# First loads interleaved with the modulation columns, W_v in quarters, two row norms on ScalarE, and a new seeded issue order

## The chip, the cores and the metric

The kernel runs on one core of a Trainium2 chip. The metric is the device time of one execution in microseconds (us). Five engines work side by side, each through its own queue in order: PE (TensorE: matmuls and transposes, with the weight loads shown as PEld), DVE (VectorE), ACT (ScalarE), POOL (GpSimd) and SP (SyncE, which here only issues DMAs). POOL and ACT issue some DMAs too.

## The reference

Two adaLN blocks on x of shape 1 x 2048 x 1024: linear attention (32 heads), then a gated feed-forward of inner size 3584. Both normalised inputs are scaled and shifted by rows that come out of the conditioning vector c.

```
mod = (silu(c) @ w_mod)            # six rows: sa, ca, ga, sb, cb, gb
h   = layernorm(x) * (1 + ca) + sa
q, k, v = h @ wqkv
o   = (phi(q) @ (phi(k)^T v)) / (phi(q) @ sum phi(k))   # per head, not causal
x   = x + ga * (o @ wo)
h   = layernorm(x) * (1 + cb) + sb
out = x + gb * (gelu(h @ w_gate) * (h @ w_up)) @ w_down
```

## The kernel before, in words

The 2048 rows are four blocks of 512, each of four row tiles of 128. Weights and rows are two-byte types. K and V of blocks 1 to 3, Q, and the feed-forward are computed with seven instead of eight block products (the helper `seven`, and lines L1492, L1503, L1698, L1742), so most of the vector work is sums of blocks (L672, a helper that all of them share).

Every instruction is first recorded by a `Plan`. PE keeps the order in which it was recorded. For DVE, ACT, POOL and SP the plan makes the order: it sweeps forwards and backwards over its own costs (`sweep`, `cost`), gives every instruction a due time, then shifts the due times of randomly chosen instructions, once for each number in `SEEDS` (`nudge`), and issues by due time. `plan.chain` makes a list of loads due in this order at the latest stage before the shifts; `plan.pairs` does so for two instructions; `aim` adds a wish without a wait.

The change sits in `start_phase`, block 0. It goes through these steps:

- **Loads** on SP: row tiles x0 to x3 (L665, 256 KB each); c (L660, 2 KB); the weights of the modulation row ca in four parts a0 to a3 (`ModRow`, L717, 512 KB each); W_v (L669) as two loads for its left half and one for its right half; the weights of row sa in four parts (L717); the left half of W_k (L669). Between them stand the row tiles x4 to x7 of block 1.
- **c chain**: transpose of c (L821), then silu of it on DVE and ACT (L822 to L825, L823, a product), and its spread over 32 columns, `srep` (L827).
- **Row norms** of the four tiles: `ln_stats` (two bn_stats, L750, and bn_aggr, L752, on DVE), `act_rstd` (L763, L764 on ACT), and the normalised rows `xh` (L771 on DVE).
- **Transposes** of each tile on PE (`start_tile`, L784), copied out of PSUM half by DVE (L787) and half by ACT (L788).
- **Modulation row ca**: four steps of four 32-column matmuls (L744), the row copied to SBUF (L730), turned into columns by four small matmuls (L735), and 1 added (L737, `opcA`).
- **V of block 0**: W_v scaled by `opcA` row by row (`scale_wv`, L792, eight instructions per half), `v_plain` (eight matmuls of 512 columns for one tile and one half, L799) and the copy out (L801). `psV0` hands out six PSUM banks in turn.
- **Row sa** the same way (L744, L730, L735, L737), then the scaled and shifted rows `hr1[0]` (L859) and the K products of block 0 (L1077).

`keep_warm` (L778) issues a matmul whose result nobody reads.

The recorded order on PE before is: transposes of tile 0, one keep_warm, ca step 0, transposes of tile 1, step 1, transposes of tile 2, steps 2 and 3, two keep_warm, the column matmuls, V left half of tiles 0 and 1, transposes of tile 3, V left half of tiles 2 and 3, V right half of tiles 0 and 1, the sa steps.

Of the kernel before, what the change touches and what calls it, by code (L numbers as in the profile page):

```python
# [24 lines left out]
class Plan:  # L25
# [170 lines left out]
    def sweep(self, back, key, look=False):  # L196
# [71 lines left out]
    PICK, NOISE = 21, 0  # L268
    SEEDS = (
        4048537842, 3052119424, 4119006662, 2336656596, 161731228, 3577097872, 1617916839, 1027230142,  # L270
        2673589267, 73385933, 3790190337, 2882579725, 3216820374, 320986960, 3784414771, 3580079639,
        2189647628, 1050075471, 3651447201, 167525183, 3753044056, 1395098839, 224573371, 585647736,
        4225116052, 2021886637, 2917317861, 1866056072, 1639904768, 1711702630, 3190854802, 40189043,
        2881217943, 3677486799, 3357445821, 867604809, 2076543648, 3896752996, 2934333674, 3357422997,
        3152768862, 640924042, 3205461639, 2011937210, 2000349924, 510719398, 2589235319, 1194506681,
        3024436697, 3992814688, 1998719246, 2949966658, 3489443318, 3776796425, 1276645235, 535667422,
        3611704417, 3250731288, 464907758, 1351614301, 2356189972, 234302744, 2220809080, 57131370, 642075108,
        2961538208, 2297863551, 4063326422, 2349725752, 2911337299, 1282626583, 2452324637, 621185154,
        7574608, 3707275484, 1951561619, 3730337220, 3301158178, 4291313931, 2153977638, 3028307953,
        3915374427, 2816343381, 3760783167, 781283501, 684728118, 501548599, 4094990745, 1484049200,  # L280
        2465562289, 3925350256, 965746493, 3646756344, 2285859381, 951057912, 2699291817, 1987664980,
        828984993, 2974115349, 2994019667, 2209336521, 2805814643, 1656178862, 2847076462, 974581971,
        2142746714, 1022025168, 2698599094, 1162505135, 294243250, 1388198210, 1320376692, 2717840438,
        1907634470, 1870354662, 3787058490, 2887567034, 731842052, 2849907486, 1949569065, 1725002371,
        3649967808, 2266963320, 1265187588, 320693273, 4133481684, 1239374557, 3322962508, 1823520108,
        922999944, 3964342922, 1626190444, 4021997209, 2818356799, 2606551328, 551488695, 2768152965,
        3756739242, 1178895203, 47899462, 2776984886, 1257449296, 978079115, 3512939827, 87745206, 2026573507,
        2193115765, 3542705403, 1987802722, 1329001258, 3298082478, 3301134813, 2791482809, 2941169553,
        2037818865, 1512528319, 2616816450, 362595370, 4022497973, 4049411141, 491327928, 2936576588,
        1810659750, 889849638, 4021601455, 3490155913, 707422581, 675677434, 1582781747, 3132129914,  # L290
        2734898311, 581041313, 3390668725, 1668609171, 617184354, 1308446589, 1521476646, 3271485029,
        188006670, 196406370, 1356859221, 673239658, 2473417458, 420321949, 3512578292, 2549304534,
        2893442801, 387476433, 320168298, 3725832190, 1491054289, 2258738015, 1870276432, 3456880632,
        2454290386, 3129029018, 697926410, 621392321, 2950830990, 3367784966, 1118316371, 2730688569,
        3949532447, 3051750465, 3325784910, 2506054308, 3860860484, 1996768650, 146936465, 1394849734,
        1876122295, 1648619962, 3935016806, 3537560656, 3783972569, 2354335454, 3477199748, 2926709925,
        16337124, 2717926436, 111481476, 3577080921, 1071120771, 2167836348, 4168772393, 3890589730,
        1077032086, 2081322183, 4253998603, 454015642, 4275186283, 4016079109, 3218202660, 304743196,
        2680513899, 3809773594, 567496057, 2830818904, 4138745561, 2171552190, 2973774733, 3221767405,
        3429062779, 1717540271, 22671747, 2877177301, 1539209414, 3279346260, 3479982363, 2042908008,  # L300
        2691901471, 1368355222, 326783083, 3723025629, 2456071862, 1765522499, 900449391, 1646784865,
        722122970, 3247420172, 144709712, 2707653883, 819893754, 3046126564, 2348285467, 1753457520,
        1370081680, 4241638063, 1889876362, 1719498627, 1097949531, 3059158255, 1826487528, 1087746401,
        1584062846, 450375441, 2497503536, 2423138386, 2114108004, 1214742892, 2086856895, 2411766887,
        2415497461, 1729688547, 1133947453, 3006387686, 18939909, 1126925613, 3055188306, 3624713728,
        1058512297, 2394622115, 3371373593, 178052737, 2641212401, 975232369, 1895527715, 3119219689,
        990010943, 2089507856, 2983971879, 996022692, 633189698, 1722843049, 1661576060, 1671655858,
        3182414464, 3582944425, 3047952838, 3254601484, 766187531, 914803382, 3727478657, 859608898,
        3197076401, 3401594207, 2518788814, 3045052436, 2880430921, 1855916904, 140371746, 1156500991,
        233814336, 3510688714, 4262759723, 1426092211, 3905079655, 2119269929, 2032944984, 3620558725,  # L310
        70133820, 3962811033, 754667546, 3073760965, 536237857, 4153583377, 4284871881, 273231253, 1032161433,
        3182043479, 2860624928, 2238869687, 1732234667, 1505353138, 2695169420, 1565396801, 3427962107,
        2673563735, 1099624156, 1397927899, 2237693769, 4118473817, 743005469, 3650425116, 2542140114,
        1153909673, 166372149, 3940934504, 2349500002, 3545793644, 410007833, 239392513, 894185139,
        1551465807, 1117651798, 1520533204, 20822420, 255004653, 438863435, 3129891357, 524023302, 4064637033,
        727558290, 1435463954, 53854510, 1999773738, 3466071934, 3199073121, 327427378, 1779665881,
        1915856973, 4162782897, 2466834344, 4248796843, 3211208784, 1624193377, 587107055, 1005140328,
        1097668263, 73267186, 3975834741, 3768422863, 2803021489, 2934859460, 2836787835, 2162329013,
        84326441, 3297589317, 913014749, 1570435363, 1768180507, 2744141746, 2458210240, 2303409726,
        786567120, 3437488657, 3085600183, 3596682727, 3241489828, 611671851, 4134240813, 1638792729,  # L320
        2540069415, 1263333970, 1713977921, 357095461, 642318044, 2476538737, 4111826224, 2345300137,
        3436573261, 2171236867, 3576962286, 4085290716, 1475585222, 3880589866, 4044342256, 3195652808,
        242737988, 3054416890, 1177578839, 3130838368, 4121588194, 29435970, 2881609414, 383494457, 726370357,
        90512414, 1561079870, 259102355, 1885219044, 2597283077, 909078396, 2293166713, 773209620, 717523002,
        1886363894, 2803820692, 507968540, 2979773247, 1603412096, 743301268, 3145502576, 2077775722,
        1338496569, 2126159865, 4004174970, 3665873461, 2555642967, 3607417742, 1860314205, 2467844904,
        1748351400, 3294511372, 1624161033, 11758325, 222342824, 1168818158, 1172645835, 3429412630,
        3380506841, 2739542149, 3442006596, 2772742892, 3321567846, 524445811, 364298885, 2556615645,
        2210968172, 2755680416, 1077432423, 4142317391, 2910697880, 2231545948, 1568488390, 2869103753,
        3579796744, 2673130065, 463737951, 1142281096, 2782314832, 2368998753, 1177439293, 2514790928,  # L330
        3029867465, 4224343348, 783400272, 2761726704, 1707892459, 3928657622, 2807650960, 992989999,
        4272533469, 3780895192, 3781928225, 200333331, 2996317106, 2825851012, 3989423859, 3739561707,
        3291555177, 1526625601, 1464234896, 2690896832, 3681443511, 713813461, 1057540405, 521674988,
        3204357066, 366938346, 2232734869, 2666123288, 707110826, 2810732530, 4204494926, 1885679090,
        1760645537, 1948061084, 2593472540, 1930019129, 1841665968, 2411340693, 4281658996, 2799186656,
        924293513, 1109206859, 3625276106, 3661854190, 1051793210, 235176749, 652886144, 3809779388,
# [68 lines left out]
def kernel(  # L405
# [305 lines left out]
    class ModRow:  # L711


        def __init__(self, m, wm, before={}):
            self.wm, self.ps, self.loads = wm, None, []
            for i in range(0, KD, 2):
# [3 lines left out]
                if i in before:  # L720
                    plan.aim(before[i])
# [1208 lines left out]
```

## Time and profile before

| what | us |
|---|---|
| median of 4 runs (lowest, highest) | 745.91 (745.42, 746.45) |
| the profiled execution | 744.84 |
| span of that execution, first to last instruction | 742.7 |
| PE busy in the span | 725.9 (98%) |
| DVE, ACT busy | 592.5 (80%), 433.1 (58%) |
| first V matmul of block 0 (L799) | at 16.38 |
| first sa step (L744 x16) | at 27.78 |
| first K product of block 0 (L1077) | at 32.32 |

Times in the tables and listings count from the start of the span. A timeline line gives start, duration, engine, source line, operation, out<-in, how many instructions it merges, and in brackets the idle time of the engine before it with what ended it. A window line gives busy time of each engine (and instruction counts), the granted PE clock, the DMA share and the GB/s that the DMA engines moved.

### The profile page before, as it was taken

How to read it: one execution, taken by the hardware profiler on the slowest of the kernel's cores; microseconds unless marked ns; L12 is line 12 of the kernel's file. 1: busy time of each engine (PE TensorE's matmuls, PEld its weight loads, DVE VectorE, ACT ScalarE, POOL GpSimd, SP SyncE). 2: the span in 40 equal slices, each digit the busy share in tenths (PEclk: the TensorE clock that was granted, in tenths of full speed). 3: DMA queues.
4: the chain of work that ended last, by engine and by line, in shares of the span. 5: the costliest groups of instructions: out<-in, count | busy, mean ns of one | idle time of the engine just before them, and what ended most of it. 6: DMA issues, size and time to landing. Idle time of an engine off the chain costs nothing.

```text
span 742.7 us, 11428 instructions
## 1 busy us (share of the span) xinstructions
PE 725.9 (98%) x4150; PEld 388.2 (52%) x4164; DVE 592.5 (80%) x1258; ACT 433.1 (58%) x757; POOL 95.0 (13%) x163
## 2 busy tenths in 40 slices
PE   4999999999999999999999999999999999999997
PEld 1444545444444455455455586545555555548664
DVE  6899987577785898698997888759788988888853
ACT  2665676669763769987876424027777777731000
POOL 2331335020001013242310000000000000000000
PEclk9999999999999999999999999999999999999999
DMA  9977159959999967998669998653231322499722
GB/s 307 330 211 226 61 144 205 312 148 277 281 273 254 340 209 251 296 242 260 193 191 236 238 264 265 228 183 125 75 114 57 113 73 99 134 280 285 291 85 71
DMA packets 151832, 152.79 MB, mean 206 GB/s; under 512 B 33824, under 2 KB 128544, under 8 KB 150496
## 3 DMA queue, kind: packets, MB, share of 16 engines
q1 hardware_dynamic: 128832, 122.44, 53.6%
q0 software_dynamic: 20592, 27.53, 15.8%
q10 hardware_dynamic: 2352, 2.10, 0.8%
q8 instruction: 32, 0.52, 0.3%
q14 instruction: 24, 0.20, 0.1%
HBM read 123.34 MB, written 36.04 MB: 215 GB/s over the span
## 4 chain that ended last, share of the span: by engine, by line
PE 93%; DVE 2%; DMA 2%; ACT 1%; issue 1%; SPq 0%; DVEq 0%
PE psum L1492 35%; PE psum L1698 13%; PE psum L1742 9%; PE psum L1503 8%; PE psum L978 8%; PE psum L1370 7%; PE psum L1048 5%; PE psum L1077 4%; PE psum L799 2%; DMA mem<-in_B_w_gate_dram 1%; PE psum L1092 1%; DVE mem L672 1%; DMA mem<-in_A_x_dram 1%; PE psum L689 0%; DVE mem L750 0%
## 5 line engine op out<-in xcount | busy, mean ns | idle before, releaser
L672 DVE TENSOR_TENSOR mem<-mem 128x512 f16<-128x512 f16 (+9 forms) x669 | 310.5, 506 | 31.6 <-ACT mem L923 11.9
L1492 PE MATMUL psum<-mem 128*128 128x512 f16 x1248 | 298.4, 379 | 0.2
L923 ACT ACTIVATE mem<-psum 128x512 f16<-128x512 f32 (+3 forms) x284 | 154.1, 563 | 111.0 <-PE psum L1742 39.8
L672 DVE TENSOR_TENSOR mem<-psum,mem 128x512 f16<-128x512 f32 (+4 forms) x204 | 154.9, 766 | 64.6 <-ACT mem L923 20.5
L1492 PEld LDWEIGHTS <-mem 128*128 128x128 f16 (+1 forms) x1248 | 122.1, 98 | 110.7 <-issue 0.7
L1698 PE MATMUL psum<-mem 128*128 128x512 f16 (+2 forms) x458 | 99.0, 372 | 0.7 <-DVE mem L672 0.5
L1503 PE MATMUL psum<-mem 128*128 128x256 f16 x560 | 89.6, 272 | 0.2 <-DVE psum L672 0.2
L1503 PEld LDWEIGHTS <-mem 128*128 128x128 f16 (+1 forms) x560 | 54.8, 98 | 44.4 <-issue 1.7
L1698 PEld LDWEIGHTS <-mem 128*128 128x128 f16 x462 | 45.2, 98 | 49.8 <-issue 0.7
L1742 PE MATMUL psum<-mem 128*128 128x256 f16 (+1 forms) x588 | 66.1, 273 | 0.0
L1742 PEld LDWEIGHTS <-mem 128*128 128x128 f16 x588 | 57.5, 98 | 9.2
L978 PE MATMUL psum<-mem 128*128 128x512 f16 (+1 forms) x272 | 61.6, 379 | 0.4
L1546 ACT ACTIVATE psum<-psum 128x512 f32<-128x512 f32 x56 | 32.8, 586 | 46.9 <-PE psum L1492 28.5
L1370 PE MATMUL psum<-mem 128*128 128x512 f16 x256 | 56.0, 379 | 0.0
L1048 PE MATMUL psum<-mem 128*128 128x512 f16 x224 | 51.2, 379 | 0.3 <-DVE mem L672 0.3
L672 DVE TENSOR_TENSOR psum<-psum,mem 128x256 f32<-128x256 f32 x80 | 34.3, 429 | 15.1 <-ACT mem L923 14.5
L978 PEld LDWEIGHTS <-mem 128*128 128x128 f16 x280 | 27.0, 98 | 31.2
L1370 PEld LDWEIGHTS <-mem 128*128 128x128 bf16 x256 | 24.8, 98 | 30.4 <-DVE mem L672 0.7
L1563 ACT ACTIVATE mem<-psum 128x512 f16<-128x512 f32 x56 | 32.6, 596 | 8.0 <-PE psum L1492 7.8
L1048 PEld LDWEIGHTS <-mem 128*128 128x128 f16 (+1 forms) x224 | 21.5, 98 | 27.7 <-issue 2.9
L1573 ACT ACTIVATE mem<-mem 128x512 f16<-128x512 f16 x56 | 34.5, 625 | 0.9 <-DVE mem L672 0.8
L1157 POOL DMA_DIRECT2D ts<-in_B_w_down_dram x28 | 31.3, 1469 | 11.6 <-DMA ts<-in_B_w_down_dram 11.2
(133 smaller groups left out, 526.0 us busy)
## 6 DMA issues: line engine op xcount, KB each, us to landing
mem<-in_B_w_gate_dram SPq DMA_DIRECT2D x14, 1024.0 KB, 5.2
mem<-in_B_w_up_dram SPq DMA_DIRECT2D x14, 1024.0 KB, 6.8
mem<-in_w_mod_dram SPq DMA_DIRECT2D x24, 512.0 KB, 6.3
mem<-ts SPq DMA_DIRECT2D x6, 1792.0 KB, 6.9
mem<-in_A_x_dram SPq DMA_DIRECT2D x32, 256.0 KB, 7.6
ts<-in_B_w_down_dram POOLq DMA_DIRECT2D x28, 256.0 KB, 7.1
mem<-ub SPq DMA_DIRECT2D x16, 448.0 KB, 5.0
mem<-in_B_w_down_dram SPq DMA_DIRECT2D x12, 448.0 KB
```

Of the source, the lines that this page charges most:

```text
L672: ve.tensor_tensor(out=out, in0=a, in1=b, op=op)
L923: ac.activation(out=t, in_=ps, func=AF.Copy)
L978: te.matmul(ps, lhsT=A[:, k, i * P:(i + 1) * P], rhs=B[:, k, :], start=(start and k == 0), stop=(k == KH - 1), skip_group_check=True)
L1048: te.matmul(o, lhsT=W[:, k, (j0 + i) * P:(j0 + i + 1) * P], rhs=h_form(a, k), start=(start and k == 0), stop=(k == KH - 1), skip_group_che ...
L1370: te.matmul(psw[:, half, :], lhsT=pqT[b][:, g, tl * P:(tl + 1) * P], rhs=Wp[:, g, half * NW:(half + 1) * NW], start=(g == 0), stop=(g == K ...
L1492: te.matmul(ps, lhsT=a[:, k, e, :], rhs=b[:, k, :], start=(start and k == 0), stop=(k == KH - 1), skip_group_check=True)
L1503: te.matmul(ps, lhsT=self.x[a][:, k, :], rhs=self.y[y][:, k, :], start=(start and k == 0), stop=(k == KH // 2 - 1), skip_group_check=True)
L1546: ac.activation(out=z, in_=x, func=AF.Copy)
L1563: ac.activation(out=o, in_=ps, func=AF.Gelu_apprx_tanh)
L1573: ac.activation(out=o, in_=o, func=AF.Gelu_apprx_tanh)
L1698: te.matmul(psm[:, q, c], lhsT=A[:, i, q * P:(q + 1) * P], rhs=wt[:, i, c], start=(start and i == 0), stop=(i == NPR - 1), skip_group_chec ...
L1742: te.matmul(ps[:, q, :], lhsT=a[:, k, q * P:(q + 1) * P], rhs=y[:, k, :], start=(start and q == 0 and k == 0), stop=(k == NPR // 2 - 1), s ...
```

## The change

- The four ca parts, the row tiles, c and W_v are loaded in one chained order, `START_LOADS`. W_v's left half is loaded as two quarters of 256 columns (v0, v1), its right half as one load (v2). The aims between single loads are gone.
- Tiles 2 and 3 are normalised with sums from ACT: `act_stats`, which the kernel already uses later on (L1300 to L1303), two passes over the row with a running sum, then log and exp. DVE loses bn_stats and bn_aggr for them.
- PE order: keep_warm, ca step 0, transposes of tile 0, ca steps 1 to 3, transposes of tile 1, columns; then V of tiles 0 and 1 on the first quarter, transposes of tile 2, V of tiles 0 and 1 on the second quarter, V left half of tile 2, transposes of tile 3, V left half of tile 3. From V right half of tile 0 on, PE's order is as before.
- `PICK`, `NOISE` and `SEEDS` are new, so the issue order of the other engines changes in the whole kernel.

```diff
-    PICK, NOISE = 21, 0
+    PICK, NOISE = 15, 2
     SEEDS = (
...
-    def ln_rows(xt):
+    def ln_rows(xt, by_act):
+        xh = xh_ring()
+        if by_act:
+            nmean, rstd = act_stats(xt)
+            ve.tensor_scalar(out=xh, in0=xt, scalar1=nmean, scalar2=rstd[:, 0:1], op0=ALU.add, op1=ALU.mult)
+            return xh
         mv = ln_stats(xt)
...
-    def scale_wv(n):
+    def scale_wv(c):
         for kd in range(KD):
-            ve.tensor_scalar_mul(out=Wvs[:, kd, n * NW:(n + 1) * NW], in0=Wv[:, kd, n * NW:(n + 1) * NW],
-                                 scalar1=opcA[:, kd:kd + 1])
+            ve.tensor_scalar_mul(out=Wvs[:, kd, c], in0=Wv[:, kd, c], scalar1=opcA[:, kd:kd + 1])
...
+    START_LOADS = "c a0 x0 a1 x1 a2 a3 v0 x2 v1 x3 v2".split()
...
-        ca = ModRow(1, wm_ca, {0: loads[0], 2: loads[1], 4: loads[2], 6: loads[3]})
-        load_w(Wv[:, 0:KH, 0:NW], 2 * D, NW, 0, KH)
-        load_w(Wv[:, KH:KD, 0:NW], 2 * D, NW, KH, KD)
-        load_w(Wv[:, :, NW:D], 2 * D + NW, NW)
-        plan.chain.append(plan.ops[-1])
+            loads[f"x{tt}"] = plan.ops[-1]
+        ca = ModRow(1, wm_ca)
+        loads.update((f"a{i}", op) for i, op in enumerate(ca.loads))
+        for name, c in (("v0", slice(0, HB)), ("v1", slice(HB, NW)), ("v2", slice(NW, D))):
+            load_w(Wv[:, :, c], 2 * D + c.start, c.stop - c.start)
+            loads[name] = plan.ops[-1]
+        plan.chain += [loads[name] for name in START_LOADS]
...
-        for i in range(KH):
-            if i < 3:
-                start_tile(halves[i % 2], i, xh[i])
-            if i == 0:
-                keep_warm(1, NW)
+        keep_warm(1, NW)
+        ca.step(0)
+        start_tile(halves[0], 0, xh[0])
+        for i in range(1, KH):
             ca.step(i)
+        start_tile(halves[1], 1, xh[1])
         ca.columns(opcA, 1.0, lambda: keep_warm(2, NW))
-        scale_wv(0)
-        for tl in range(TT):
-            v_plain(tl, 0)
-            if tl == 1:
-                start_tile(halves[1], 3, xh[3])
-        scale_wv(1)
+        scale_wv(slice(0, HB))
+        for tl in range(2):
+            v_plain(tl, 0, slice(0, HB))
+        scale_wv(slice(HB, NW))
+        start_tile(halves[0], 2, xh[2])
+        for tl in range(2):
+            v_plain(tl, 0, slice(HB, NW))
+        v_plain(2, 0)
+        start_tile(halves[1], 3, xh[3])
+        v_plain(3, 0)
+        scale_wv(slice(NW, D))
         v_plain(0, 1)
         v_plain(1, 1)
```

`act_stats` and the changed `v_plain`:

```python
def act_stats(xt):
    nmean, ssq, rstd = sum_ring(), sum_ring(), rstd_ring()
    ac.activation(out=junk_wo, in_=xt, func=AF.Copy, scale=-1.0 / D, accum_out=nmean)
    ac.activation(out=junk_wo, in_=xt, func=AF.Square, bias=nmean, accum_out=ssq)
    ac.activation(out=rstd, in_=ssq, func=AF.Ln, bias=eps5, scale=1.0 / D)
    ac.activation(out=rstd, in_=rstd, func=AF.Exp, scale=-0.5)
    return nmean, rstd

def v_plain(tl, n, c=slice(0, NW)):
    if c.start == 0:
        v_banks[tl, n] = psV0()
    ps = v_banks[tl, n]
    for k in range(KD):
        te.matmul(ps[:, c], lhsT=hs0[:, k, tl * P:(tl + 1) * P], rhs=Wvs[:, k, n * NW + c.start:n * NW + c.stop],
                  start=(k == 0 and c.start == 0), stop=(k == KD - 1), skip_group_check=True)
    if c.stop == NW:
        v_out(tl, n, ps)
```

## Prediction

> **What bounds the kernel now.** I read the engines' busy times first, then PE's waits, then the first 35 us of the timeline, then windows for the DMA rate.
>
> ```profile
> PE 725.9 (98%) x4150; PEld 388.2 (52%) x4164; DVE 592.5 (80%) x1258; ACT 433.1 (58%) x757; POOL 95.0 (13%) x163
> ...
> PE psum L784 <- DVE mem L771: 6.1, 1, 6.1
> PE psum L821 <- DMA mem<-in_c_dram: 3.7, 1, 3.7
> PE psum L799 <- DVE mem L792: 0.6, 1, 0.6
> PE psum L1698 <- DVE mem L672: 0.5, 1, 0.5
> ```
>
> PE is the bound. Of 16.8 us without PE work (742.7 - 725.9), 9.8 lie before its first transposes; no single wait after the start is over 0.5. So whatever moves the first sa step (27.78) moves the end, and later stages have hardly a microsecond to give back, but can lose.
>
> ```profile
> 6.26 0.69 DVE L750 BATCH_NORM_STATS2 mem<-mem 128x6 f32<-128x512 bf16 x1 [1.17 <-DMA mem<-in_A_x_dram]
> 10.76 0.69 DVE L750 BATCH_NORM_STATS2 mem<-mem 128x6 f32<-128x512 bf16 x1 [0.83 <-DMA mem<-in_A_x_dram]
> 11.37 0.53 DVE L771 TENSOR_SCALAR mem<-mem 128x1024 f16<-128x1024 bf16 x1
> 14.75 0.67 DVE L730 CAST mem<-psum 128x512 f16<-128x512 f32 x1
> 16.38 4.11 PE L799 MATMUL psum<-mem 128*128 128x512 f16 x16 [0.65 <-DVE mem L792]
> 19.48 1.40 DVE L792 TENSOR_SCALAR mem<-mem 128x512 f16<-128x512 bf16 x5 [0.85 <-DMA mem<-in_A_wqkv_dram]
> 20.33 0.61 PE L784 MATMUL psum<-mem 128*128 128x128 f16 x8
> 20.78 7.07 PE L799 MATMUL psum<-mem 128*128 128x512 f16 x32
> 27.78 1.05 PE L744 MATMUL psum<-mem 128*32 128x512 bf16 x16
> ```
>
> Tile x1 arrives at 6.26, x3 at 10.76. DVE stands in order: the norm of tile 1 (11.37) waited behind x3's statistics, though its own were ready at 8.1. From the row copy to the first V matmul is 1.63 us. PE is dense from there to 27.78, 11.4 us. The right half of W_v arrives at 19.48, five microseconds before PE wants it.
>
> ```profile
> 4.00:5.00 1.00, 0.00 (x0) 0.00 (x0) 1.00 (x4) 0.21 (x1) 0.77 (x4) 1.00 0.54 141
> 5.00:6.00 1.00, 0.00 (x0) 0.00 (x0) 0.09 (x2) 0.00 (x0) 0.00 (x0) 1.00 0.92 338
> 14.00:16.00 2.00, 1.33 (x14) 0.35 (x15) 1.73 (x6) 0.99 (x3) 0.00 (x0) 1.00 1.10 347
> 22.00:24.00 2.00, 2.00 (x11) 0.88 (x9) 1.97 (x6) 0.60 (x1) 0.19 (x1) 1.00 1.05 387
> 443.00:447.00 4.00, 4.00 (x25) 2.25 (x23) 4.00 (x6) 0.60 (x1) 0.00 (x0) 1.00 0.94 232
> ```
>
> The last two numbers are DMA share and GB/s. The start is at the DMA limit from 5 us on: 347 while W_v comes in rows of 1 KB, 387 with rows of 2 KB. In 443 to 447 parts of w_down with rows of 512 bytes are loaded, and the engines, as busy, move 232.
>
> **The skill.** The Trainium skill, "DMA: Bandwidth & Descriptors", section "Queues, rings and completion order", says that one DMA is spread over up to 16 rings, each served in order, so a load is done when its slowest ring is. The trace agrees: 1.05 MB had moved by 6 us (sum of the windows), twice what ends with x1, yet x1 was released at 6.26. I use measured releases, moved by the bytes put ahead of them. The same page's "Specifications" give 512 bytes as the smallest transfer at line rate; here 512-byte rows reached only 232. "TensorE: Matmul & The Clock Gate", Part 1, has PE at half clock for its first 3.4 us of work; the trace agrees (eight transposes: 1.03 at 9.98, 0.62 at 13.38). The changed start is cold in the same way.
>
> **The change, part by part.**
>
> *Loads.* SP's new order is x0, a0, x1, c, a1, a2, a3, x2, v0, x3, v1, v2, then the sa parts and x4 to x7 mixed, W_k. Half a megabyte (a0) goes ahead of x1: 0.52 / 0.35 = 1.5 us, less up to 0.5 if the half-idle stretch at 4 to 5 us fills. x1 at 7.5 (6.3 to 8.0). v0 and v1 have rows of 512 bytes: 1.05 MB at 232 instead of 347 is 4.5 instead of 3.0, +1.5 us (+0.3 at 319, read at 402 to 404; +2.9 at 177, read at 387 to 390). All bytes up to v2 are the same as before, so v2 comes at 19.48 + 1.5 - 0.3 = 20.7, v1 at about 17.6, x2 at 12.4.
>
> *c chain and first norms.* DVE's new order is statistics of x0 and x1, then the c chain with the two norms between its parts. From 7.5: two bn_stats to 8.8, c copied and aggregate 9.05, exp on ACT and hand-over, add at 9.65, norm 10.1, reciprocal, second norm 10.65, product and spread 11.05. PE: ca step 0 at 11.15, cold 0.45; transposes of tile 0, 0.86 cold; three steps at 0.45, 13.85; row copy 14.05. To the first V matmul 1.63, and 0.3 because tile 1's transposes and DVE's copy of them now stand in between: 16.0. Before: 16.38. That gain is 0.4: c and x1 later take back what no longer waiting for x3 gives.
>
> *V stage.* PE's work is the same but for the transposes of tile 2, which now come after the first V matmul: +0.45. Thirty-two matmuls of 256 columns take the place of sixteen of 512; such a chain runs at 109 ns each (168 in 18.34), so nothing changes. The first V group is paced by eight scalings as before. The norm of tile 2 comes from ACT: x2 at 12.4; 1.06 + 0.19 + 1.15 + 0.19 + 0.29 + 0.20 = 3.1, with two copies of 0.6 between and a wait for tile 1's transposes, so DVE has it at 17.4 and finishes at 17.9; the scaling of v1 stands behind it on DVE, 17.95 to 19.5. PE: V on v0, 16.0 to 18.4; transposes of tile 2 to 18.85; V on v1, held by the last scaling, to 20.55; tile 2 to 22.3; transposes of tile 3 to 22.75. Then V of tile 3 follows directly: it waits for DVE's copy (0.2 + 0.42 + 0.08), which before was hidden behind tile 2's matmuls, +0.7. On DVE that copy stands behind seven scalings of v2 (1.9 us from 20.7: 22.6), just in time. Then 1.73 and 3.46: the sa steps at 28.65, +0.9. The sa loads, 1.2 us later than before, are just in time too. DVE's 3.1 us saved statistics (four of 0.68, two of 0.20) cost nothing and gain nothing, since DVE waits for loads here; ACT's added 6.2 us lie in its idle time except as counted.
>
> *New issue order.* PE's order after the start is untouched; I followed the other engines' new orders against the trace's durations, and list where something now stands ahead of work with no slack. One place: at the first Wo products (L1370, 186.7) DVE's four products for them (L672, 184.52 to 187.0) now have three instructions of an earlier phi ahead of them (0.42 + 0.69 + 0.69), and ACT two (2.2 us) which before ran at 177 to 182. DVE's idle time there, 0.96, takes up part: +0.7 (0 to 1.0). A wait of 0.3 at 178.5 goes (-0.2), about +0.1 elsewhere. In the tail the last residual load (x2s, L1682) is issued only after a store that DVE's order delays by 7 us. From store issue to this load's issue the trace has 2.3 us, and 2.9 from there to landing, so it lands at about 735 and is needed at 736.3: +0.1 for two sums placed late.
>
> Sum: +0.9 + 0.7 - 0.2 + 0.1 + 0.1 = +1.6. The profiled span goes from 742.7 to 744.3 and its execution from 744.84 to 746.4. The runs' median lies 1.07 above that execution; I add the sum to the median: 747.5, rounded up to 747.6, as the extra waits are more likely to add than to cancel.
>
> **Rivals.** (1) *The start gets shorter.* Deciding is x1. If the mixed loads fill the early gap and it lands by 6.3, everything before V moves up by 1.2 to T = 14.8, and with v1 at 17.0 the stage ends near 27.6: -0.2, in all +0.5, 746.4. If the PE and DVE chain is shorter still, first V at 13.5, and the 512-byte rows run at 319, sa starts at 26.1 and the kernel ends 1.2 to 1.7 earlier: 744.3. For it: the norm of tile 1 loses a wait of 3 us. Against: x1 has twice the bytes ahead. The line to a gain is a first V matmul below about 14.5. (2) *W_v becomes the bound.* At 177 GB/s v2 lands at 22.1; seven scalings, tile 3's copy, 5.2 of matmuls: sa at 29.8, +2.0, in all 748.7. For it: those two w_down loads. (3) *The new order breaks something later*, above all the tail load, whose margin is 1.2 us; each microsecond beyond it is one at the end: 751.
>
> **Chances.** Forecast 0.45 (its own range 746.5 to 748.6), about the same by rival 1 0.17, faster by rival 1 0.13, rival 2 0.17, rival 3 0.08. A difference under 0.2% (1.5 us: 744.4 to 747.4) can't be told from none by measurement. Slower: 0.28 of the forecast's 0.45, and rivals 2 and 3, 0.53; same 0.17 + 0.17 = 0.34; faster 0.13. The range from 744.6 to 750.0 leaves out the lower half of the fast case and most of rival 3.
>
> **What would show it.** Right: first step of ca (L744) near 11.2, first V matmul near 16.0, a new PE wait of 0.7 before tile 3's V matmuls on DVE's copy, the sa steps after 28.3, W_v waited for later than 19.48, a new stall of 0.5 or more near 187. Wrong: x1's statistics before 6.5, a first V matmul before 15, sa steps before 27.5, or PE idle later than 200 us for more than 1 us.

## The result and the profile after

The changed kernel takes 747.12 us (median of 44 executions, 744.98 to 753.70), the kernel before, timed beside it, 745.88 (62 executions, 744.18 to 748.76). The ratio is 1.0025, 95% interval 1.0015 to 1.0034. The profiled execution took 746.04, its span is 744.1, with PE busy for 726.7. Line numbers are now those of the changed kernel: L1425 was L1370, L711 was L672, L781 was L744, L843 was L799, L1180 (loads of the denominators) was L1125.

PE's waits in the changed kernel (us in total, times, longest):

```profile
PE psum L871 <- DMA mem<-in_c_dram: 6.0, 1, 6.0
PE psum L781 <- DMA mem<-in_w_mod_dram: 2.4, 1, 2.4
PE psum L843 <- DVE mem L833: 1.8, 1, 1.8
PE psum L1425 <- DVE mem L711: 1.6, 2, 1.4
PE psum L1753 <- DVE mem L711: 0.5, 1, 0.5
```

There are two new ones: 1.8 before the first V matmul, and 1.6 at the Wo products (L1425), 1.4 of it in one piece. The timeline of the start:

```profile
5.74 1.29 DVE L787 BATCH_NORM_STATS2 mem<-mem 128x6 f32<-128x512 bf16 x2 [0.75 <-DMA mem<-in_A_x_dram]
9.12 0.62 PE L781 MATMUL psum<-mem 128*32 128x512 bf16 x4 [2.41 <-DMA mem<-in_w_mod_dram]
12.15 0.69 DVE L767 CAST mem<-psum 128x512 f16<-128x512 f32 x1 [1.42 <-PE psum L781]
12.86 1.06 PE L819 MATMUL psum<-mem 128*128 128x512 f16 x2
14.24 1.66 DVE L833 TENSOR_SCALAR mem<-mem 128x256 f16<-128x256 bf16 x8
15.76 1.91 PE L843 MATMUL psum<-mem 128*128 128x256 f16 x16 [1.75 <-DVE mem L833]
22.33 5.35 PE L843 MATMUL psum<-mem 128*128 128x512 f16 x24 [0.30 <-DVE mem L828]
27.61 1.05 PE L781 MATMUL psum<-mem 128*32 128x512 bf16 x16
```

x1 is there at 5.74, the ca row is copied at 12.15, 2.6 us earlier than before. At the first V matmul 0.6 of this is left, at the sa steps 0.17. The timeline at the Wo products of the second block of rows:

```profile
187.58 1.72 SPq L1180 DMA_DIRECT2D mem<-den  x4
...
200.28 1.90 DVE L711 TENSOR_TENSOR mem<-mem 128x1024 bf16<-128x1024 bf16 x3 [4.99 <-DMA den<-mem]
...
202.09 1.00 DVE L1364 TENSOR_SCALAR mem<-mem 128x1024 f16<-128x1024 bf16 x2
...
203.01 0.68 DVE L711 TENSOR_TENSOR mem<-mem 128x1024 bf16<-128x1024 bf16 x1
...
203.61 1.21 DVE L711 TENSOR_TENSOR mem<-psum,mem 128x1024 bf16<-128x1024 f32 x1
...
204.87 1.46 PE L1425 MATMUL psum<-mem 128*128 128x512 f16 x6 [1.36 <-DVE mem L711]
```

SP issues the four loads of the denominators of block 1 at 187.58; the last of them lands at 200.16. ("den<-mem" in the bracket names a store that shares a semaphore with one of these loads.) VectorE stands idle for 5 us until 200.28, multiplies phi(q) by them (four L711 of 128x1024 without PSUM), with two layer-norm outputs (L1364) in between, and only then empties the PSUM bank that PE wants. PE wanted it at 203.5 and stood idle for 1.36.

| place | before | after | difference |
|---|---|---|---|
| first sa step | 27.78 | 27.61 | -0.17 |
| 32 matmuls of a modulation step at 201 us | 201.71 | 201.60 | -0.11 |
| next Wo product | 203.56 | 204.87 | +1.31 |
| end of the span | 742.7 | 744.1 | +1.4 |

So the whole loss of the profiled execution is the wait at 203. The start came out even in this execution. Between the sa steps and 201 us nothing is left over either: the new stall at 187, where PE starts 0.8 late in two pieces, is paid by stalls of the kernel before at 163.5, 175.2 and 178.1 (0.3, 0.2 and 0.5) that are gone.

### The profile page after: what moved, and what is told of

Same layout as the page of the kernel before. It is cut to its first block, busy times and chain, and to the rows that moved or that the text cites. A ratio compares the mean times of both kernels' runs of the same rounds, so it can differ in the third digit from the quotient of the medians.

```text
span 744.1 us, 11467 instructions
## 1 busy us (share of the span) xinstructions
PE 726.7 (98%) x4166; PEld 390.2 (52%) x4180; DVE 589.9 (79%) x1260; ACT 437.5 (59%) x765; POOL 97.9 (13%) x163
## 4 chain that ended last, share of the span: by engine, by line
PE 92%; DVE 3%; DMA 2%; ACT 1%; issue 1%; SPq 0%; DVEq 0%; ACTq 0%
PE psum L1547 35%; PE psum L1753 13%; PE psum L1797 9%; PE psum L1558 8%; PE psum L1033 8%; PE psum L1425 6%; PE psum L1103 5%; PE psum L1132 4%; PE psum L843 2%; DVE mem L711 2%; DMA mem<-den 1%; PE psum L1147 1%; DMA mem<-in_w_mod_dram 1%; PE psum L781 1%; PE psum L825 0%
## 5 line engine op out<-in xcount | busy, mean ns | idle before, releaser
L711 DVE TENSOR_TENSOR mem<-mem 128x512 f16<-128x512 f16 (+11 forms) x669 | 309.4, 506 | 30.5 <-ACT mem L978 14.8
L711 DVE TENSOR_TENSOR mem<-psum,mem 128x512 f16<-128x512 f32 (+4 forms) x204 | 154.9, 766 | 68.2 <-ACT mem L978 25.2
L1425 PE MATMUL psum<-mem 128*128 128x512 f16 x256 | 56.2, 379 | 1.9 <-DVE mem L711 1.6
L711 DVE TENSOR_TENSOR psum<-psum,mem 128x256 f32<-128x256 f32 x80 | 34.2, 428 | 13.5 <-ACT mem L978 12.8
L1425 PEld LDWEIGHTS <-mem 128*128 128x128 bf16 x256 | 24.8, 98 | 32.6 <-issue 2.1
```

The costliest lines, as they stand in the source:

```text
L711: ve.tensor_tensor(out=out, in0=a, in1=b, op=op)
L1425: te.matmul(psw[:, half, :], lhsT=pqT[b][:, g, tl * P:(tl + 1) * P], rhs=Wp[:, g, half * NW:(half + 1) * NW], start=(g == 0), stop=(g == K ...
```

## Experiments

Each kernel below issues from a written-out list: that of the changed kernel (or of the kernel before, where it says so) with the stated moves alone. Ratios are to the kernel before, timed beside it on the same chip; a profiled execution stands for itself, and single executions turned out to differ by several microseconds.

| kernel | median us | ratio, 95% interval | profiled span |
|---|---|---|---|
| start_only | 746.33 | 1.0012 (0.9998 to 1.0025) | 745.7 |
| rest_only | 746.16 | 1.0013 (1.0003 to 1.0024) | 744.2 |
| evict_first | 747.29 | 1.0014 (1.0001 to 1.0026) | 745.2 |
| mod_early | 746.36 | 1.0009 (0.9998 to 1.0020) | 743.7 |
| three_moves | 749.79 | 1.0047 (1.0031 to 1.0062) | 747.1 |
| kd_order | 747.18 | 1.0013 (0.9999 to 1.0028) | 746.8 |
| old_loads | 749.66 | 1.0051 (1.0031 to 1.0071) | 746.4 |
| no_warm | 747.25 | 1.0012 (0.9988 to 1.0036) | 744.8 |
| after_mods | 745.49 | 0.9991 (0.9981 to 1.0001) | 742.9 |
| before_mods | 745.13 | 0.9980 (0.9970 to 0.9991) | 743.7 |
| after_mods_kd | 745.00 | 0.9980 (0.9971 to 0.9989) | 742.7 |
| best | 744.84 | 0.9983 (0.9973 to 0.9992) | 743.2 |

**The start alone, the order alone.**

```diff
 start_only: issue order of the changed kernel's start
-then the changed kernel's order
+then the kernel before's order
```

> The start of the changed kernel, followed by the issue order of the kernel before for everything after it. My theory now: the start is neutral and the time is lost later. First sa step at 27.6 us, no wait over 0.3 at 203 us, span 742.5 (0.2 below before), ratio 0.9995 to 1.0005. The sum that I predicted with had +0.9 for the start: it would give span 743.6, ratio 1.001.

```diff
 rest_only: issue order of the kernel before's start
-then the kernel before's order
+then the changed kernel's order
```

> The start of the kernel before, followed by the issue order of the changed kernel. If the order after the start is the loss: span 744.2, a PE wait of 1.3 to 1.5 us at about 203.5 on a VectorE eviction, and the same few executions some 5 us longer as the changed kernel has. If the loss needs the changed start: span 742.7, no wait at 203.

rest_only did what was expected: span 744.2, PE waits 1.24 at 204.47 for the same eviction. The changed start isn't needed for the loss. start_only had its sa steps at 27.66, but its span was 745.7, not 742.5. In the profiled execution PE lost 1.1 and 1.4 us at 186 to 188 and 1.1 at 205, although the order there is that of the kernel before: VectorE had to wait for the denominators until 186.66 and 202.62, where the kernel before began these products at 184.52 and 199.36. Issue order on VectorE alone doesn't explain that; the transfers come at different times in different executions. The two ratios, 1.0012 and 1.0013, don't tell the parts apart. That of start_only lies nearer to the 1.001 of the predicted sum than to the theory's 1.0005, and its interval holds both. So the start is neutral as far as single profiles show it (sa steps at 27.50 to 28.00 in the six with the changed start as it is, at 27.50 to 28.80 in the three with the old one); what it costs the median is open.

**VectorE's order or the late transfer.**

```diff
 evict_first: VectorE from 195 us
+eviction of row tile 2 (L711)
 products with the denominators 0, 3, 2 (L711)
-two layer-norm outputs (L1364)
 product 1 (L711)
-eviction of row tile 2 (L711)
+two layer-norm outputs (L1364)
```

> The changed kernel with one PSUM eviction, which was ready at 198.4 us, put ahead of the four multiplications by the denominators in VectorE's order, and two layer-norm outputs put behind them. If VectorE's order makes the wait at 203: the multiplications end at 200.28 + 4 x 0.60 + 0.08 = 202.8, before PE asks for them at 203.5; the wait falls from 1.4 to under 0.2 us, span 742.8. If the late transfer alone makes it: the wait stays over 1 us, span 744.

```diff
 mod_early: SP
+one 512 KB load of w_mod (L720) at 171 us
 ...
-one 512 KB load of w_mod (L720) at 184.2 us
 four loads of the denominators (L1180)
```

> The changed kernel with one 512 KB load of modulation weights moved on SyncE from 184.2 us back to 171 us, where the kernel before had it. If its bytes ahead of the denominators' loads make these late: VectorE is released 0.9 us earlier, at 199.4, and the wait at 203 falls from 1.4 to 0.5, span 743.2. If the loads are late because they are issued 0.54 us later: release at 200.2 as in the changed kernel, span 744.1.

Timeline of evict_first, VectorE and PE:

```profile
202.44 2.50 DVE L711 TENSOR_TENSOR mem<-mem 128x1024 bf16<-128x1024 bf16 x4 [1.97 <-DMA mem<-den]
...
204.44 1.81 PE L1425 MATMUL psum<-mem 128*128 128x512 f16 x7
```

The denominators came even later, at 202.44, and PE still didn't wait: with the eviction done early, PE needs only the first of the four products. So VectorE's order makes the wait at 203 as long as it is. The span was 745.2 all the same, because this execution lost 1.0 and 0.8 us at 186 to 188 and 1.4 at 243 to other late loads. In mod_early VectorE was released 11.80 us after the issue of the first of the four loads, 12.70 in the changed kernel, and PE's wait fell from 1.36 to 0.49, as expected. But only 0.33 of this is an earlier release (199.95 for 200.28, expected 199.4); for the rest PE asked 0.55 later in this execution. So evict_first shows VectorE's half of the cause, and the half of the transfers isn't shown by mod_early; it is by after_mods below. Each move alone leaves the ratio where it can't be told from the changed kernel's.

**All moves at once, and one too many.**

```diff
 three_moves: evict_first and mod_early together, and VectorE from 183 us
+four products with the denominators (L711)
 two instructions of the next phi (L973, L711)
-four products with the denominators (L711)
```

> The changed kernel with three moves: the eviction ahead of the multiplications at 200 us (as in evict_first), the modulation load back to 171 us (as in mod_early), and the four multiplications at 185 us ahead of two instructions of the next phi. Theory, VectorE's order and the late load make both waits: the wait at 187 falls from 0.8 to about 0.4 (ScalarE's part stays), that at 203 to under 0.2, span 742.4, ratio to the kernel before 0.9985 to 1.0005. Rival, the loads vary so much from execution to execution that order decides little: a wait of over 0.8 somewhere between 185 and 206, ratio over 1.001.

It was slower, 1.0047. Timeline of three_moves, ScalarE and PE:

```profile
188.60 1.06 ACT L1063 ACTIVATE mem<-mem 128x1024 f16<-128x1024 f16 x1 [2.73 <-DVE mem L711]
...
192.62 5.30 PE L1425 MATMUL psum<-mem 128*128 128x512 f16 x16 [2.54 <-ACT mem L1073]
```

The products didn't start earlier than in the changed kernel (184.93 against 185.06), since their load had only just come (VectorE idle 1.21 on it). But the phi instructions now behind them held ScalarE back by 2.6 us, and PE waited 2.54 for its eviction. PE went on at full speed for 1.1 us after that wait; then eight or so matmuls of 512 columns came 0.43 apart instead of 0.216, from 193.74 to 197.15: about 1.7 us more. A third move that looked like a gain on VectorE cost more than the two others could bring.

**The transfers moved out of the crowd.** Windows of the changed kernel:

```profile
150.00:156.00 6.00, 6.00 (x58) 3.33 (x57) 4.22 (x7) 5.57 (x6) 1.45 (x2) 1.00 0.29 115
...
166.00:200.00 34.00, 33.49 (x178) 14.50 (x171) 23.88 (x39) 30.63 (x39) 0.09 (x1) 1.00 1.05 271
```

From 166 to 200 us the DMA engines are full, with the denominators near the end of the queue (in the kernel before the share is 1.04). Ahead of them in this stretch are eight loads of w_mod, 4 MB, whose buffers are free from 146.6 to 158.1 (in after_mods SP issues them from 146.9 to 158.5). The engines have room for part of that time: their share is 0.05 and 0.03 in 152 to 156 and 0.04 in 162 to 164, near 1 or above in 146 to 150 and 156 to 160. SP can't issue the loads: it stands at an x load (L1420) until 163.9.

```diff
 after_mods: SP from 142 us
+eight 512 KB loads of w_mod (L720)
 two x loads (L1420), wait until 163.9
 ...
-eight 512 KB loads of w_mod (L720), 166 to 184 us
```

> The changed kernel with one move on SyncE: the eight 512 KB loads of modulation weights, issued from 166 to 184 us behind an x load that waits until 163.9, go ahead of that x load; their buffers are free from 146.6 to 158.1 us, when the DMA engines are nearly idle. If the queue of transfers from 166 to 200 us makes the denominators late: these are there when VectorE comes to them at about 195.3, the wait of 5 us on VectorE and the PE wait at 203 go, the one at 187 (0.8) stays, span 742.6, ratio to the kernel before 0.9975 to 0.9995, and executions over 749 us are rare. If VectorE's order alone makes the wait: it stays near 1 us, span 744.

> The same move in the kernel before. Its profile has no wait at 203 to lose, so its span stays at 742.5 to 742.9; but if late transfers spread its executions (744.1 to 748.8), the median comes down towards the fastest: 745.0, ratio 0.998 to 0.9995. If not: ratio 1.000.

Windows of after_mods:

```profile
150.00:156.00 6.00, 6.00 (x59) 3.36 (x56) 4.20 (x8) 5.32 (x6) 1.45 (x2) 1.00 0.94 338
...
166.00:200.00 34.00, 33.49 (x177) 14.52 (x177) 26.13 (x42) 30.61 (x39) 1.93 (x1) 1.00 0.81 200
```

and its timeline at the products:

```profile
195.41 0.68 DVE L711 TENSOR_TENSOR mem<-mem 128x1024 bf16<-128x1024 bf16 x1
```

The share falls from 1.05 to 0.81, VectorE finds the denominators when it comes to them (195.41, expected 195.3), and the PE wait at 203 is gone with VectorE's order as it was. Span 742.9, ratio 0.9991; no execution of 22 is over 749, where the changed kernel, timed in another session, had 10 of 44. The same move in the kernel before gives 0.9980. Its own profile had shown no wait there, and its profiled span with the move is no shorter (743.7: in that execution the start ran late, sa steps at 28.80). Its median fell from 746.25 to 745.13. That fits late denominators costing the kernel before about a microsecond too, in other executions than the profiled one; these weren't traced.

The landing times say it most plainly. In the ten profiles without this move the last of the four loads landed 10.9 to 13.7 us after the first was issued, in the four with it 6.5 to 6.9. Not all of the difference is bytes ahead: a load counts its semaphore up in sixteen parts, and in the changed kernel fifteen parts of the last load had landed at 198.75, the sixteenth at 200.16. This lag of one part is 0.2 to 2.8 us in the ten and under 0.1 in the four; why one part lags isn't shown.

**The start.**

```diff
 kd_order: VectorE at 14 us, scalings of W_v's first quarter by block of rows
-3, 5, 7, 1, 4, 2, 0, 6
+0, 1, 2, 3, 4, 5, 6, 7
```

> The changed kernel with the first eight scalings of W_v on VectorE put in the order in which PE uses them (0 to 7); in the changed kernel block 0 is scaled seventh, and PE's first V matmul waits for it. First V matmul at 14.6 instead of 15.76, first sa step at 27.1 instead of 27.61. If the end follows the start: span 743.6. If the denominators' transfer takes it back: the wait at 203 grows by 0.5 to 1.9, span 744.1.

```diff
 old_loads: SP
-x0, a3, x1, c, a2, a0, a1, x2, v0, x3, v1, v2
+x0, c, x1, x2, a3, a2, x3, a0, a1, v0, v1, v2
```

Here the four parts have the names by which the ca steps use them (step 0 needs a0). The prediction, and the expectation that follows, name them by their place in the queue. The kernel before has a1, a0, x3, a2, a3.

> The changed kernel with its first twelve loads in the old sequence (x0, c, x1, x2, a0, a1, x3, a2, a3, then W_v in its three parts). My prediction held that a0 ahead of x1 costs x1 1.2 us: then x1's statistics start before 5.74 here and the first sa step is at 27.6 or earlier. If the new sequence is what starts the ca steps early: c is read at 3.7, but the first ca step comes at 10.9 instead of 9.12, first V matmul at 17.2, first sa step at 28.7.

```diff
 no_warm
-        ca.columns(opcA, 1.0, lambda: keep_warm(2, NW))
+        ca.columns(opcA, 1.0)
```

> The changed kernel without the two matmuls on scratch data between the ca row's copy and the column matmuls (they keep PE busy and go into no result). If they stand in the way: column matmuls at 13.1 instead of 13.71, first V matmul at 15.15 instead of 15.76, first sa step at 27.1. If what follows is set by the loads or by VectorE: sa step still at 27.6.

Timeline of old_loads:

```profile
12.25 0.62 PE L781 MATMUL psum<-mem 128*32 128x512 bf16 x4 [7.97 <-DMA mem<-in_w_mod_dram]
...
30.73 1.05 PE L781 MATMUL psum<-mem 128*32 128x512 bf16 x16
```

x1's statistics start at 5.08 in it, so a0 ahead of x1 costs x1 0.66 us. But the first ca step waits for its weights until 12.25, and the sa steps come at 30.73, 3.1 us later than in the changed kernel; the ratio is 1.0051. Not all of that is the sequence by kind. The run keeps the changed kernel's order among the four parts, in which step 0 needs the third, and this landed at 12.20, behind x3; the second, which step 0 needs in the kernel before, had landed at 10.16. With that order of the parts the sa steps would have come about 2 us earlier, near 28.7 (an estimate from these landings), as the expectation had it. So the interleaved sequence is worth about 1 us by this estimate, and the rest of the changed start gives that back; the kernel before's own sequence under the changed PE order wasn't run.

In kd_order PE's wait for the scalings fell from 1.75 to 0.58, as expected, and yet the sa steps came at 29.10: PE ran at half speed until 19.3 us (the 16 V matmuls took 3.57 instead of 1.91), and c itself came 0.7 later in this execution. no_warm had its column matmuls at 12.73, its first V matmul at 14.76 (expected 15.15), half speed until 18.1, and sa steps at 28.23. In both, what was gained before V was lost to PE's speed in V. The change of PE's pace fell anywhere from 12.6 to 19.3 us in the profiles of these kernels.

**Together.**

```diff
 after_mods_kd: after_mods and kd_order
```

> after_mods with the first scalings of W_v in PE's order as in kd_order. If nothing takes the start's gain back now: first V matmul at 14.6, sa step at 27.1, span 742.1, ratio 0.997 to 0.999. What decides in the start may be when PE comes to full speed: from 12.8 to 19.3 us in the profiles so far; if PE is slow to 18 us or later, sa step after 28 and no gain over after_mods.

```diff
 best: after_mods_kd, and at 184 us
 ScalarE
+L1194 eviction that PE asks for first
 L1194 eviction that PE asks for second
-L1194 eviction that PE asks for first
 VectorE
-products with the denominators 0, 2, 1, 3
+products with the denominators 0, 1, 2, 3
```

> after_mods_kd with two swaps before the first Wo products at 186 us: on ScalarE the eviction that PE asks for first goes ahead of one that it asks for later, and on VectorE the second multiplication in PE's order goes ahead of the third. If these two orders make the wait at 187 (0.3 on ScalarE, 0.2 on VectorE, 0.8 with what follows): it falls under 0.3, span 742.1, ratio to the kernel before 0.997 to 0.9985. If VectorE's three phi instructions ahead of all four multiplications make it, as I predicted: 0.4 or more stays, span 742.5.

after_mods_kd had its first V matmul at 14.07 and sa steps at 27.04 in its profile, span 742.7. PE's waits in best:

```profile
PE psum L843 <- DVE mem L833: 0.6, 1, 0.6
PE psum L1753 <- DVE mem L711: 0.5, 1, 0.5
PE psum L843 <- DVE mem L828: 0.3, 1, 0.3
```

No wait at L1425 is left: the stall of 0.8 at 187 is gone with the three phi instructions still ahead of the products. Its span, 743.2, is 0.5 longer than after_mods_kd's because its sa steps came 1.4 later, at 28.42, with PE at half speed until 18.4 us. The medians 745.00 and 744.84 and their intervals can't be told apart. Both kernels beat the kernel before, beside which they were timed, by 0.2%, and by their intervals the changed kernel too. So does before_mods, so this margin is the transfers' move, and no run shows that the changed start adds to it.

## Why the prediction came out as it did

The time was right and its make-up was not. The sum said +1.6 for the profiled execution, and +1.2 was measured (span +1.4). The median's distance from that execution, taken over as 1.07, was 1.08 again; with executions spread over almost 9 us that is luck. Of the signs named for being right, the first V matmul near 16 and the stall near 187 came; of those for being wrong, x1's statistics before 6.5 and PE idle after 200 did. Step by step:

- **Loads.** x1 at 7.5 (6.3 to 8.0) was wrong: 5.74. The base was misread. In the kernel before the tile that ends VectorE's wait at 6.26 is x2, which landed at 6.24 and whose statistics were ready at 8.1. VectorE takes it ahead of x1, which had landed at 4.22; x1's statistics are the next line:

  ```profile
  8.04 1.23 DVE L750 BATCH_NORM_STATS2 mem<-mem 128x6 f32<-128x512 bf16 x2
  ```

  So x1 did not have twice its bytes moved before its release, and the norm of tile 1 lost a wait of about 1.3 us, not 3 (ready at 10.08, done at 11.37). The 1.5 us for a0's bytes ahead of x1 came out between the two profiles: 5.71 is 1.49 after 4.22, although the gap at 4 to 5 us filled (398 GB/s, 141 before); against old_loads it is 0.66. Rival 1 had x1 as its deciding point, "lands by 6.3", and from it sa steps near 27.6, and they came at 27.61. It started from the same misread base, and its first V at 14.8 was 15.76, so part of that is luck too. With x1 early the c chain was through at 8.9, and the first ca step started at 9.12, when its weights came, for 11.15 predicted.
- **W_v in 512-byte rows** was mis-sized. The rate of 232 was read from another stretch; at 14 to 16 us the engines moved 305 to 343. VectorE scaled v1 from 16.37 and v2 from 19.25 without a wait for them (17.6 and 20.7 predicted). Rival 2 fell with it.
- **Row copy to first V matmul**, 1.93 by the prediction, took 3.61, and this failed as mechanism. "The first V group is paced by eight scalings as before" doesn't hold: the new order on VectorE scales block 0 seventh, so PE waits for nearly all of them: from the columns (L774, 14.04) to V it is 1.72 us, 0.60 before. The two keep_warm matmuls and the transposes of tile 1 stand ahead of the column matmuls at half speed: from the copy's start to these it is 1.56, 0.73 before. This hid how early x1 was: first V at 15.76 for 16.0.
- **V stage.** The 0.7 for tile 3's copy was 0.46, of it 0.30 as a wait on L828, in the place named. In all the start was -0.17 where +0.9 stood in the sum.
- **New order at 187**, +0.7, was 0.8: the right place and size, the wrong cause. It is which eviction ScalarE and which product VectorE does first (best makes both swaps at once, so their shares aren't separated), not the three phi instructions ahead; to move the products ahead of two of them makes it worse (three_moves). The waits near 178 went, as said, and with those at 163.5 and 175.2 they were worth 1.0 where the sum had 0.2. So the stretch from the sa steps to 201 us, +0.6 in the sum, came to +0.06. The tail load cost nothing, as said.
- **What was missed** is the wait at 203, +1.4. I followed the new orders with each load landing a fixed time after its issue. In a stretch with a DMA share of 1.05 it doesn't: the four loads took 10.9 to 13.7 us from issue to the last landing. The margin could have been read in the profile of before:

  ```profile
  199.36 1.29 DVE L672 TENSOR_TENSOR mem<-mem 128x1024 bf16<-128x1024 bf16 x2 [3.65 <-DMA den<-mem]
  ...
  202.23 1.22 DVE L672 TENSOR_TENSOR mem<-psum,mem 128x1024 bf16<-128x1024 f32 x1
  ...
  203.56 2.76 PE L1370 MATMUL psum<-mem 128*128 128x512 f16 x12
  ```

  VectorE's eviction ended at 203.45 and PE used the bank at 203.56, 0.1 us later, after VectorE had been idle 3.65 on a DMA. Rival 3 had the kind of loss and the wrong place.

So the forecast stood on errors that cancel: +0.9 for a start that is even, +0.6 for a stretch up to 201 us that is even, and nothing for a wait of 1.4. That the time was right is luck. This holds for the profiled execution; what the start does to the median is left open by start_only.

## What to carry to other kernels

Don't give a load one latency. Here the same four loads of 1 MB in all landed 12.6 us after the first issue in a stretch with a DMA share of 1.05, and 6.5 after it where earlier loads had been moved away (0.81). Look where the DMA engines are full for the consumer with no margin, and look in the stretch before it for loads whose buffers are already free but which stand in the issuing queue behind one that waits. Before the order of a queue is improved by hand, ask who waits for the instructions that are put behind. Match a wait to its load by the semaphore, not by the order in which the loads are listed: x2 was taken for x1 here. And one profiled execution can show no wait where the others have one: the median's distance from it is worth an explanation.

## What was not expected of the hardware

- PE lost its pace after a wait of 2.54 us in three_moves: it went on at full speed for 1.1 us, then ran at half speed for 3.4. The window over it, with a mean granted clock of 0.83:

  ```profile
  190.00:200.00 10.00, 7.46 (x39) 2.78 (x38) 6.44 (x9) 6.85 (x9) 0.00 (x0) 0.83 0.92 236
  ```

  The Trainium skill, "TensorE: Matmul & The Clock Gate", Part 1, has half clock only after an idle window of about 3.4 us; here a shorter wait was enough. Waits of 1.1 to 1.6 at 203 and of 1.75 before the first V matmul did not do it in the profiles. This would explain the changed kernel's ten executions over 749 us, all of them with a mean granted clock of 0.997 or 0.998, as three_moves has in its profile (0.997): the denominators late enough, and the wait costs 1.7 us more. These executions were not traced, so that is argued, not shown; evict_first, whose profile has no wait at 203, also has two executions at 0.998. What is shown is that with the loads moved none of 22 was over 749.
- The same page has the activity window "free-running", not tied to the kernel's start. The traces agree: in all fourteen profiles every closed stretch of full speed in the clock record is a whole number of steps of 3.413 us (212 to 214 of them, in three_moves 53 before the drop, one at half speed, and 161 after it). PE came to full speed between 12.6 and 19.3 us. Counted back from that moment in such steps, PE was idle for at most 0.43 us in the last step and for at least 0.58 in the one before it, in every profile; the step before the drop in three_moves had 2.29 idle. So where the steps fall against PE's gaps would set the moment. That was read from these traces afterwards, and no run controls it; what an earlier V is worth is left open with it.
